# Decoding float64 weights with a parametric Relu, and splitting them on GpSimd, in a fused attention and MoE kernel

## The chip, the cores and the metric

The kernel runs on one core of a Trainium2 chip. The metric is the device time of one execution in microseconds (us). The core has five engines with instruction queues of their own, each worked off in order: TensorE (PE, with its weight loads shown apart as PEld), VectorE (DVE), ScalarE (ACT), GpSimd (POOL) and SyncE (SP, which issues the DMAs here). An instruction that has to wait holds up everything behind it in its own queue.

## The reference

Two layers in a row, without biases. For 8 batches and 8 heads with 576 positions and head size 64, thresholded softmax attention; then, on the 4608 tokens of width 512, a two-layer perceptron with SiLU.

```python
scores = q @ k.T / sqrt(64)
scores = where(scores >= max(scores) - tau, scores, -1e9)
attn = softmax(scores); x = attn @ v            # heads side by side: 4608 x 512
h = x @ w_in                                    # 512 x 2048
out = (h * sigmoid(h)) @ w_out                  # 2048 x 512
```

`q`, `k`, `v` are float32. `w_in` and `w_out` come as float64 numbers.

## The kernel before

**Weights.** They are loaded as pairs of 32-bit words, in 32 pieces of 128 x 512 (16 of `w_in`, then 16 of `w_out`). `decode_weights(i)` makes a float32 of each pair in the buffer `wst`. POOL multiplies the upper word, read as a float32, by 2^-112 (L179). DVE shifts the bits of this left by three (L183), which drops the sign, and ors in the top bits of the lower word (L186). PE multiplies a matrix of ones with the upper 16 bits of all four blocks of the piece (L197). The sums over four pieces bound the magnitudes, and DVE takes their maximum (L202). ACT makes the sign from the upper word (L204) and POOL multiplies it in (L205).

`pow2_scales` makes a power of two out of such bounds by a few operations on one column on DVE; for `v` it first takes the maximum over the partitions (a diagonal matrix by ACT, a matmul with ones on PE, a reduction on DVE). For the weights this was not needed, as the matmul with ones has already summed over the partitions. `split_weights(i)` then writes a high part in float16, scaled by ACT (L211), and a low part in float16, the scaled value less the high part, by DVE (L212). All this happens in one buffer: a split piece lies two slots ahead of the decoded one, so the high part of piece i may be written only once the split of piece i-2 has read its source.

**Attention.** A tile is 128 rows of scores. There are 288: first 16 of batch 0 (whose scores and products take float32 directly), then 20 of batch 0, then 36 for each further batch. Per tile PE makes the scores (L400 for the first 16, L412), DVE the maximum (L422), ACT the exponential (L432), DVE the threshold and the sum (L441), ACT the division (L454). For all but the first 16, the weights of the tile are split in two float16 parts: the high one by ACT, from the 9th of these tiles on by POOL (L465), the low one by POOL (L468 and L471); a DMA transposes them (`wT<-hl`), and PE multiplies them with `v` (L496). POOL also makes the low parts of the keys (`klo`, L326) and, in batch 0, of the queries (`qstack`, L311). The buffers of a tile's weights number four, those of its scores two, so a late step soon holds up the steps ahead of it.

**MoE.** `h_unit` (L539, 12 matmuls each) and `o_unit` (L570, 48 matmuls per output block) run on PE between the tiles. Each takes the high and the low part of the weights. A unit needs the weights' two parts, and the tokens' `x16`, made from the attention's output.

**What sets the order.** The program is written tile by tile, with a plan for the weights (`W_PLAN`: load, decode, scale, split at given tiles) and priorities. A scheduler then lays the instructions into the five queues by these priorities and by its own estimate of when each is ready. The order in the queues is fixed when the program is built. A change of one operation so moves others.

Of the kernel before, what the change touches and what calls it, by code (L numbers as in the profile page):

```python
# [52 lines left out]
def attention_moe(  # L53
# [51 lines left out]

    def pow2_scales(mx, name, across=True):

# [3 lines left out]
        nc.vector.tensor_reduce(out=one, in_=mx, op=ALU.max, axis=AX.X)  # L111
        if across:


            diag = const.tile([P, P], BF16, name=f"{name}_diag", tag="diag")
            nc.scalar.activation(diag, ident, AF.Copy, scale=one)
            allp = bank([P, P], f"{name}_ps", 0 if turn[1] == 3 else None)
            nc.tensor.matmul(allp, ones, diag, start=True, stop=True)
            one = const.tile([P, 1], F32, name=f"{name}_all", tag=f"{k}_all")
            nc.vector.tensor_reduce(out=one, in_=allp, op=ALU.max, axis=AX.X)  # L120
        cl = const.tile([P, 1], F32, name=f"{name}_cl", tag=f"{k}_cl")
        nc.vector.tensor_scalar(
            out=cl, in0=one, scalar1=2.0**-20, scalar2=2.0**47, op0=ALU.max, op1=ALU.min
        )
        e2 = const.tile([P, 2], I32, name=f"{name}_e2", tag=f"{k}_e2")
        nc.vector.tensor_scalar(
# [45 lines left out]
    def decode_weights(i):  # L172


        t = wraw.pop(i)
        low, top = t[:, :, 0], t[:, :, 1]
        w = wst[:, i + WSPARE, :]
        wbits = w.bitcast(I32)
        nc.gpsimd.tensor_scalar(  # L179
            out=w, in0=top.bitcast(F32), scalar1=2.0**-112, scalar2=1.0,  # L180
            op0=ALU.mult, op1=ALU.mult,
        )
        nc.vector.tensor_scalar(  # L183
            out=wbits, in0=wbits, scalar1=3, scalar2=None, op0=ALU.logical_shift_left
        )
        nc.vector.scalar_tensor_tensor(  # L186
            out=wbits, in0=low, scalar=29, in1=wbits,
            op0=ALU.logical_shift_right, op1=ALU.bitwise_or,
        )


        n, c = divmod(i, 4)
        if c == 0:
            wps[n] = bank([P, P], f"wps_{n}", 2)
        upper = w.bitcast(BF16).rearrange("p (c t) -> p c t", t=2)[:, :, 1]
        for j in range(4):
            nc.tensor.matmul(  # L197
                wps[n], ones, upper[:, j * P : (j + 1) * P],
                start=(c == 0 and j == 0), stop=(c == 3 and j == 3),
            )  # L200
        if c == 3:
            nc.vector.tensor_reduce(out=wmx[:, n : n + 1], in_=wps[n], op=ALU.max, axis=AX.X)  # L202
        sg = stage.tile([P, 512], F16, tag="wsg", name=f"wsg_{i}", bufs=2)
        nc.scalar.activation(sg, top.bitcast(F32), AF.Sign)  # L204
        nc.gpsimd.tensor_tensor(out=w, in0=w, in1=sg, op=ALU.mult)  # L205

    def split_weights(i):
        w = wst[:, i + WSPARE, :]
        hi = w16[:, i, 0:512]
        sc = wsc["in" if i < 4 * NK else "out"][:, 0:1]  # L210
        nc.scalar.activation(hi, w, AF.Copy, scale=sc)  # L211
        nc.vector.scalar_tensor_tensor(  # L212
            out=w16[:, i, 512:1024], in0=w, scalar=sc, in1=hi, op0=ALU.mult, op1=ALU.subtract
        )
# [33 lines left out]
    def vscale(b):  # L248
        vsc[b] = pow2_scales(vmx[b], f"v{b}")
        if b == 0:  # L250
# [430 lines left out]
    def scale_in():  # L681
        wsc["in"] = pow2_scales(wmx[:, 0:4], "i_w", across=False)

    def scale_out():
        wsc["out"] = pow2_scales(wmx[:, 4:8], "o_w", across=False)

# [128 lines left out]
```

## Time and profile before

The time is 1250.52 us, the median of three runs (1245.27 to 1252.15). One execution was profiled.

| | |
|---|---|
| profiled execution | 1244.94 us |
| its span, first to last instruction | 1243.2 us |
| PE busy | 1140.7 us (92%) |
| DVE busy | 961.3 us (77%) |
| ACT busy | 818.0 us (66%) |
| POOL busy | 759.4 us (61%) |
| mean granted PE clock | 0.971 |

Busy shares are averages over stages of different kinds. The weights are handled in the first 190 us; the last 180 us have no attention any more. In the profile, a row of a group gives line, engine, operation, `out<-in`, the shapes, the count, the busy time in us with the mean of one in ns, and the engine's idle time just ahead of these instructions with what ended it. A row of a stretch gives its bounds and length, the busy time and count of each engine, the granted clock, the share of time that the DMA engines were busy and their GB/s.

### The profile page before, as it was taken

To read this page: it belongs to the slowest core of one execution; us is meant where nothing else is said; L and a number is where in the kernel's file an instruction comes from. 1 tells how busy PE (TensorE), PEld (TensorE's weight loads), DVE (VectorE), ACT (ScalarE), POOL (GpSimd) and SP (SyncE) were. 2 spreads that over 40 slices of the span, in tenths; PEclk is the share of its full clock that TensorE was granted. 3 is DMA by queue.
4 is the path that set the end of the run, shared out by engine and by line. 5 is a ranking of instruction groups with operands and counts; after the bars stand their busy time and mean duration, and the time that the engine had idled before them with its cause. 6 is when DMAs were issued, how large, how long until landed. Compare 5 with 4: busy or idle time off the path is not lost.

```text
span 1243.2 us, 26997 instructions
## 1 busy us (share of the span) xinstructions
PE 1140.7 (92%) x9400; PEld 897.4 (72%) x9400; DVE 961.3 (77%) x2627; ACT 818.0 (66%) x1505; POOL 759.4 (61%) x952
## 2 busy tenths in 40 slices
PE   5674879899799989999999999999999999999998
PEld 3453657676577767777888877787777877777777
DVE  7999998978888888989888957988689848333230
ACT  5787777766777667777777747776577847433331
POOL 4568988577778768786878708773688538200000
PEclk8996889899899999999999999999999999999999
DMA  9457867678868868888778638783687436200000
GB/s 297 127 177 179 186 130 146 132 151 167 151 130 145 166 133 147 148 158 172 143 140 152 137 90 154 143 148 101 110 168 148 87 73 116 54 15 16 12 14 24
DMA packets 363480, 158.15 MB, mean 127 GB/s; under 512 B 329552, under 2 KB 338256, under 8 KB 363344
## 3 DMA queue, kind: packets, MB, share of 16 engines
q1 hardware_dynamic: 363344, 156.43, 61.9%
q8 instruction: 74, 1.21, 0.4%
q14 instruction: 62, 0.51, 0.1%
HBM read 66.72 MB, written 9.44 MB: 61 GB/s over the span
## 4 chain that ended last, share of the span: by engine, by line
PE 54%; DVE 25%; DMA 6%; ACT 6%; issue 5%; POOL 4%; SPq 0%; ACTq 0%; POOLq 0%; DVEq 0%
PE o L570 20%; PE h L539 19%; PE s L412 7%; PE a L496 7%; DVE w L441 6%; DVE sm L422 5%; DMA vraw<-in_vL 3%; DVE qstack L316 3%; ACT w L432 2%; DMA wT<-hl 2%; DVE wst L212 2%; DVE h L548 1%; DVE gbuf L555 1%; ACT w L454 1%; DVE wst L186 1%
## 5 line engine op out<-in xcount | busy, mean ns | idle before, releaser
L539 PE MATMUL h<-x,wst 128*128 128x288 f16 (+2 forms) x3072 | 430.8, 290 | 12.7 <-DVE gbuf L555 10.2
L570 PE MATMUL o<-gbuf,wst 128*128 128x288 f16 (+2 forms) x3072 | 420.6, 287 | 8.2 <-ACT wst L580 6.5
L539 PEld LDWEIGHTS <-wst 128*128 128x128 f16 x3072 | 294.6, 99 | 102.0 <-issue 22.0
L570 PEld LDWEIGHTS <-wst 128*128 128x128 f16 x3072 | 293.2, 98 | 90.5 <-issue 11.4
L468 POOL TENSOR_TENSOR hl<-w,hl 128x512 f16<-128x512 f32 x272 | 329.3, 1211 | 14.5 <-ACT hl L463 2.1
L465 POOL TENSOR_SCALAR hl<-w 128x576 f16<-128x576 f32 x264 | 180.6, 687 | 190.8 <-ACT w L454 128.3
L432 ACT ACTIVATE w<-s,sm 128x576 f32<-128x576 f32 x288 | 210.5, 738 | 83.5 <-DVE sm L422 30.6
L441 DVE SCALAR_TENSOR_TENSOR w<-s,sm,w 128x576 f32<-128x576 f32 x288 | 232.0, 812 | 32.5 <-ACT w L432 30.2
L454 ACT ACTIVATE w<-w,sm 128x576 f32<-128x576 f32 x288 | 217.6, 770 | 52.4 <-DVE sm L449 49.3
L422 DVE TENSOR_REDUCE sm<-s 128x1 f32<-128x576 f32 x288 | 215.0, 749 | 31.9 <-PE s L412 28.2
L548 DVE SCALAR_TENSOR_TENSOR h<-th,h 128x288 f32<-128x288 f32 (+2 forms) x256 | 116.2, 455 | 108.5 <-ACT th L547 106.4
L547 ACT ACTIVATE th<-h,msc 128x288 f32<-128x288 f32 (+2 forms) x256 | 126.2, 497 | 106.0 <-PE h L539 104.7
L412 PE MATMUL s<-khi,qstack 128*128 128x288 f32 x608 | 158.7, 343 | 19.0 <-DVE w L441 14.5
L554 ACT ACTIVATE gbuf<-h 128x288 f16<-128x288 f32 (+2 forms) x256 | 103.5, 407 | 81.3 <-DVE h L548 80.2
L555 DVE SCALAR_TENSOR_TENSOR gbuf<-h,gbuf 128x288 f16<-128x288 f32 (+2 forms) x256 | 114.9, 451 | 40.4 <-ACT gbuf L554 39.6
L496 PE MATMUL a<-wT,v 128*64 128x288 f16 (+1 forms) x1680 | 131.3, 298 | 13.5 <-DMA wT<-hl 13.3
L412 PE MATMUL s<-klo,qstack 128*128 128x288 f32 x608 | 132.6, 300 | 0.0
L326 POOL TENSOR_TENSOR klo<-kraw,khi 128x576 fp32r<-128x576 f32 x64 | 95.2, 1487 | 56.5 <-ACT khi L324 53.8
L412 PEld LDWEIGHTS s<-khi,qstack 128*128 128x128 f32 x608 | 97.9, 196 | 41.9 <-issue 22.9
L496 PEld LDWEIGHTS <-v 128*64 128x64 f16 x1680 | 94.5, 113 | 40.1 <-issue 30.3
L412 PEld LDWEIGHTS s<-klo,qstack 128*128 128x128 f32 x608 | 100.3, 194 | 0.3
L471 POOL TENSOR_TENSOR hl<-w,hl 128x64 f16<-128x64 f32 x272 | 100.2, 368 | 0.0
(84 smaller groups left out, 866.5 us busy)
## 6 DMA issues: line engine op xcount, KB each, us to landing
qraw<-in_qT SPq DMA_DIRECT2D x128, 144.0 KB, 3.0
kraw<-in_kT SPq DMA_DIRECT2D x128, 144.0 KB, 3.0
vraw<-in_vL SPq DMA_DIRECT2D x32, 320.0 KB, 3.7
wraw<-in_w_out SPq DMA_DIRECT2D x16, 512.0 KB, 3.8
out_t<-wst SPq DMA_DIRECT2D x56, 144.0 KB, 2.2
wT<-hl SPq DMA_TRANSPOSE x304, 3.4
gbuf<-in_w_in SPq DMA_DIRECT2D x8, 512.0 KB, 7.5
wraw<-in_w_in SPq DMA_DIRECT2D x8, 512.0 KB, 6.0
```

Of the source, the lines that this page charges most:

```text
L412: nc.tensor.matmul(s_ps[:, j, :HALF], lhs, kk[:, j * HALF : (j + 1) * HALF], start=(n == 0), stop=(n == len(seq) - 1),)
L422: nc.vector.tensor_reduce(out=negm, in_=s_ps[:, :, :HALF], op=ALU.max, axis=AX.XY, negate=True)
L432: nc.scalar.activation(wtile[t].rearrange("p (j c) -> p j c", j=2), sps[t][:, :, :HALF], AF.Exp, bias=small[t][:, 0:1],)
L441: nc.vector.scalar_tensor_tensor(out=w3, in0=s_ps[:, :, :HALF], scalar=sm[:, 1:2], in1=w3, op0=ALU.is_ge, op1=ALU.mult, accum_out=sm[:, 2:3],)
L454: nc.scalar.activation(w, w, AF.Copy, scale=r)
L465: nc.gpsimd.tensor_scalar(out=fl[:, 0:S], in0=w, scalar1=1.0, scalar2=1.0, op0=ALU.mult, op1=ALU.mult)
L468: nc.gpsimd.tensor_tensor(out=fl[:, 640:1152], in0=w[:, 0:512], in1=fl[:, 0:512], op=ALU.subtract)
L496: nc.tensor.matmul(a_ps[odd * D : (odd + 1) * D, :n], vt[:, lo_v, odd, kv, :], wT[v, b * H + 2 * p + odd][:, kw, c0 - base : c0 - base + n ...
L539: nc.tensor.matmul(ph[:, :n], wi(c, f, lo_w), x16[b, lo_x][:, c, c0 : c0 + n], start=(k == 0), stop=(k == 11),)
L548: nc.vector.scalar_tensor_tensor(out=ph[:, :n], in0=th[:, :n], scalar=1.0, in1=ph[:, :n], op0=ALU.add, op1=ALU.mult,)
L555: nc.vector.scalar_tensor_tensor(out=g[:, 1, :n], in0=ph[:, :n], scalar=2.0**-14, in1=g[:, 0, :n], op0=ALU.mult, op1=ALU.subtract,)
L570: nc.tensor.matmul(ps[:, :n], wo(f, d, lo_w), g[:, lo_g, :n], start=(f == 0 and k == 0), stop=(f == NF - 1 and k == 2),)
```

## The change

The decode: ACT applies a parametric Relu to the upper word with scale 2^-112 and slope 2^32 for negative numbers. After it a negative number has a larger exponent than a positive one, such that the shift by three leaves the sign bit in place. ACT's Sign and POOL's two operations are gone; DVE's two stay.

The bound: since the values now bear a sign, PE multiplies each block with itself, transposed, instead of with ones. The maximum of the sums is taken, now over the partitions too, and its root is made by halving the exponent. So the two scales of the weights go through the diagonal, the matmul and the reduction, and through three more one-column operations.

The split: POOL scales the piece in place (L220 of the changed kernel), ACT copies the high part (L223), POOL subtracts it (L224). DVE's L212 is gone. The PSUM banks of some of the scale matmuls are others.

```diff
-    def pow2_scales(mx, name, across=True):
+    def pow2_scales(mx, name, own=None, squared=False):
...
-        if across:
-            (the five statements below, indented)
+        diag = const.tile([P, P], BF16, name=f"{name}_diag", tag="diag")
+        nc.scalar.activation(diag, ident, AF.Copy, scale=one)
+        allp = bank([P, P], f"{name}_ps", own)
+        nc.tensor.matmul(allp, ones, diag, start=True, stop=True)
+        one = const.tile([P, 1], F32, name=f"{name}_all", tag=f"{k}_all")
+        nc.vector.tensor_reduce(out=one, in_=allp, op=ALU.max, axis=AX.X)
...
+        if squared:
+            nc.vector.tensor_scalar(out=twice, in0=cl, scalar1=2.0, scalar2=None, op0=ALU.mult)
+            nc.vector.tensor_scalar(
+                out=half, in0=twice.bitcast(I32), scalar1=1, scalar2=EXPMASK,
+                op0=ALU.logical_shift_right, op1=ALU.bitwise_and,
+            )
+            nc.vector.tensor_scalar(
+                out=cl, in0=half.bitcast(F32), scalar1=2.0**64, scalar2=None, op0=ALU.mult
+            )
...
     def decode_weights(i):
-        nc.gpsimd.tensor_scalar(
-            out=w, in0=top.bitcast(F32), scalar1=2.0**-112, scalar2=1.0,
-            op0=ALU.mult, op1=ALU.mult,
+        nc.scalar.activation(
+            w, top.bitcast(F32), AF.Prelu, scale=2.0**-112, alpha=2.0**32
         )
...
         for j in range(4):
+            part = upper[:, j * P : (j + 1) * P]
             nc.tensor.matmul(
-                wps[n], ones, upper[:, j * P : (j + 1) * P],
+                wps[n], part, part,
...
-        sg = stage.tile([P, 512], F16, tag="wsg", name=f"wsg_{i}", bufs=2)
-        nc.scalar.activation(sg, top.bitcast(F32), AF.Sign)
-        nc.gpsimd.tensor_tensor(out=w, in0=w, in1=sg, op=ALU.mult)

     def split_weights(i):
-        nc.scalar.activation(hi, w, AF.Copy, scale=sc)
-        nc.vector.scalar_tensor_tensor(
-            out=w16[:, i, 512:1024], in0=w, scalar=sc, in1=hi, op0=ALU.mult, op1=ALU.subtract
+        nc.gpsimd.tensor_scalar(
+            out=w, in0=w, scalar1=sc, scalar2=1.0, op0=ALU.mult, op1=ALU.mult
+        )
+        nc.scalar.activation(hi, w, AF.Copy)
+        nc.gpsimd.tensor_tensor(
+            out=w16[:, i, 512:1024], in0=w, in1=hi, op=ALU.subtract
         )
...
-        vsc[b] = pow2_scales(vmx[b], f"v{b}")
+        vsc[b] = pow2_scales(vmx[b], f"v{b}", (None, 2)[b] if b < 2 else 0)
...
-        wsc["in"] = pow2_scales(wmx[:, 0:4], "i_w", across=False)
+        wsc["in"] = pow2_scales(wmx[:, 0:4], "i_w", squared=True)
...
-        wsc["out"] = pow2_scales(wmx[:, 4:8], "o_w", across=False)
+        wsc["out"] = pow2_scales(wmx[:, 4:8], "o_w", 2, squared=True)
```

**How the order moves.** Lines of the changed kernel from L114 on stand at most 12 lines lower. POOL's queue from its first work on the weights, before (L179 and L205 are the decode, L311 the queries' low part):

```order
L179 TENSOR_SCALAR wst<-gbuf 128x512 x2
L205 TENSOR_TENSOR wst<-wst,wsg_147 128x512
L179 TENSOR_SCALAR wst<-gbuf 128x512 x2
L179 TENSOR_SCALAR wst<-wraw_160 128x512
L205 TENSOR_TENSOR wst<-wst,wsg_157 128x512
L179 TENSOR_SCALAR wst<-wraw_222 128x512
```

and the same place in the changed program (L323 are the queries, L338 the keys, L220 the scaling and L224 the subtraction of the split, `hl_1305` the first attention tile that POOL handles, number 28 of the program):

```order
L323 TENSOR_TENSOR qstack_85<-qraw_0_1047,qstack_85 64x320
L323 TENSOR_TENSOR qstack_87<-qraw_1_1118,qstack_87 64x320
L338 TENSOR_TENSOR klo_1116<-kraw_0_1048,khi_1114 128x576
L338 TENSOR_TENSOR klo_1203<-kraw_1_1119,khi_1201 128x576
L220 TENSOR_SCALAR wst<-wst,i_w_sc 128x512 x15
L224 TENSOR_TENSOR wst<-wst 128x512
L220 TENSOR_SCALAR wst<-wst,i_w_sc 128x512
L224 TENSOR_TENSOR wst<-wst 128x512
L338 TENSOR_TENSOR klo_1353<-kraw_2_1243,khi_1351 128x576
L323 TENSOR_TENSOR qstack_85<-qraw_2_1242,qstack_85 64x320
L480 TENSOR_TENSOR hl_1305<-w_28_1230,hl_1305 128x512
```

POOL has only four instructions on queries and keys until the scale of `w_in` is there, and then 15 scalings in one go, ahead of the first attention tile.

POOL's queue again, in the changed program, where the scale of `w_out` is ready (`hl_1888` and `hl_1927` are tiles 40 and 41):

```order
L477 TENSOR_SCALAR hl_1888<-w_40_1806 128x576
L338 TENSOR_TENSOR klo_1934<-kraw_7_1826,khi_1932 128x576
L323 TENSOR_TENSOR qstack_87<-qraw_7_1825,qstack_87 64x320
L477 TENSOR_SCALAR hl_1927<-w_41_1878 128x576
L220 TENSOR_SCALAR wst<-wst,o_w_sc 128x512 x15
L224 TENSOR_TENSOR wst<-wst 128x512
L220 TENSOR_SCALAR wst<-wst,o_w_sc 128x512
L224 TENSOR_TENSOR wst<-wst 128x512
L480 TENSOR_TENSOR hl_1888<-w_40_1806,hl_1888 128x512
L483 TENSOR_TENSOR hl_1888<-w_40_1806,hl_1888 128x64
```

Before, one decode multiplication stood between the tiles here, and no scaling; now 18 instructions of the split stand ahead of the low parts of tiles 40 and 41. The other 14 subtractions follow one or two at a time between later tiles.

PE's queue at the score of the 45th scored tile (tile 57), before (L412 the score, L570 the second layer, `o_0_3` the fourth and last output block of batch 0's first columns):

```order
L570 LDWEIGHTS wst
L570 MATMUL o_0_3_1938<-gbuf,wst 128x256
L412 MATMUL s_2437<-khi_2226,qstack_87 128x288 x2
L412 MATMUL s_2437<-klo_2228,qstack_87 128x288 x2
L570 LDWEIGHTS wst
L570 MATMUL o_0_3_1938<-gbuf,wst 128x256
```

and in the changed program (L424 the score, L582 the second layer):

```order
L582 LDWEIGHTS wst
L582 MATMUL o_0_1_1580<-gbuf,wst 128x256
L424 MATMUL s_2397<-khi_2186,qstack_87 128x288 x2
L424 MATMUL s_2397<-klo_2188,qstack_87 128x288 x2
L582 LDWEIGHTS wst
L582 MATMUL o_0_0_1444<-gbuf,wst 128x256
```

At the same tile PE is now still at the first two output blocks instead of the fourth. Counted over the queues, the old one has 166 matmuls of L570 ahead of this score, the new one 82 of L582; at the 85th scored tile they differ by 12 matmuls of the first layer and no more.

More of the change, by code (lines that the diff above doesn't have):

```diff
@@ L111, in pow2_scales @@
         nc.vector.tensor_reduce(out=one, in_=mx, op=ALU.max, axis=AX.X)
-        if across:
[L115 to L120, printed above, removed]
+        diag = const.tile([P, P], BF16, name=f"{name}_diag", tag="diag")
[4 more added lines that the diff above has]
+        nc.vector.tensor_reduce(out=one, in_=allp, op=ALU.max, axis=AX.X)
         cl = const.tile([P, 1], F32, name=f"{name}_cl", tag=f"{k}_cl")
+        low, high = (2.0**-40, 2.0**94) if squared else (2.0**-20, 2.0**47)
         nc.vector.tensor_scalar(
-            out=cl, in0=one, scalar1=2.0**-20, scalar2=2.0**47, op0=ALU.max, op1=ALU.min
+            out=cl, in0=one, scalar1=low, scalar2=high, op0=ALU.max, op1=ALU.min
         )
+        if squared:
+            twice = const.tile([P, 1], F32, name=f"{name}_twice", tag=f"{k}_twice")
+            nc.vector.tensor_scalar(
+                out=twice, in0=cl, scalar1=2.0, scalar2=None, op0=ALU.mult
+            )
+            half = const.tile([P, 1], I32, name=f"{name}_half", tag=f"{k}_half")
+            nc.vector.tensor_scalar(
+                out=half, in0=twice.bitcast(I32), scalar1=1, scalar2=EXPMASK,
+                op0=ALU.logical_shift_right, op1=ALU.bitwise_and,
+            )
+            cl = const.tile([P, 1], F32, name=f"{name}_root", tag=f"{k}_root")
+            nc.vector.tensor_scalar(
+                out=cl, in0=half.bitcast(F32), scalar1=2.0**64, scalar2=None, op0=ALU.mult
+            )
         e2 = const.tile([P, 2], I32, name=f"{name}_e2", tag=f"{k}_e2")
@@ L210, in split_weights @@
         sc = wsc["in" if i < 4 * NK else "out"][:, 0:1]
-        nc.scalar.activation(hi, w, AF.Copy, scale=sc)
-        nc.vector.scalar_tensor_tensor(
-            out=w16[:, i, 512:1024], in0=w, scalar=sc, in1=hi, op0=ALU.mult, op1=ALU.subtract
+        nc.gpsimd.tensor_scalar(
+            out=w, in0=w, scalar1=sc, scalar2=1.0, op0=ALU.mult, op1=ALU.mult
+        )
+        nc.scalar.activation(hi, w, AF.Copy)
+        nc.gpsimd.tensor_tensor(
+            out=w16[:, i, 512:1024], in0=w, in1=hi, op=ALU.subtract
         )
```

## The prediction

> **What bounds the kernel now.** I began with the busy time of each engine in five stretches of the span. The columns are stretch, length, then busy time and instruction count of PE, weight load, DVE, ACT and POOL, then granted clock, DMA share and GB/s.
>
> ```profile
> 0.00:75.00 75.00, 46.47 (x245) 29.82 (x245) 63.82 (x157) 51.10 (x95) 40.23 (x46) 0.93 0.66 207
> 75.00:190.00 115.00, 79.67 (x574) 61.91 (x574) 113.26 (x259) 91.13 (x168) 94.42 (x95) 0.82 0.69 163
> 206.00:215.00 9.00, 8.29 (x65) 6.30 (x64) 8.70 (x29) 6.73 (x11) 7.65 (x11) 1.00 0.87 174
> 215.00:345.00 130.00, 110.75 (x849) 84.64 (x851) 113.24 (x319) 90.29 (x159) 93.90 (x120) 0.92 0.77 152
> 345.00:1243.00 898.00, 879.57 (x7525) 700.69 (x7521) 650.32 (x1835) 568.85 (x1058) 509.11 (x664) 1.00 0.59 112
> ```
>
> From 345 us on PE is busy 98% of the time at full clock. The work left there is the same in both programs, so the change can act only ahead of it, where PE idles 28.5 us before 75 us, 35.3 us from 75 to 190 us and 20 us from 206 to 345 us. From 75 to 190 us DVE is busy 113.26 of 115 us: it bounds that stage. POOL is second, with 94.42.
>
> Then the chain of waits, in pieces (start, length, what), of the end of that stage and what follows:
>
> ```profile
> 183.01 0.66 DVE wst L212
> 189.16 1.47 POOL hl L468
> 195.70 1.36 POOL klo L326
> 197.06 1.64 POOL hl L468
> 200.83 1.33 POOL hl L465 x2
> 209.49 1.37 POOL klo L326
> ```
>
> DVE's weight split (L212) lies on the chain until about 185 us; from 189 us POOL does. So POOL is already the next bound, before anything is moved to it.
>
> **DVE's part.** The rows of single lines give shortest, median and longest duration in ns:
>
> ```profile
> L212 DVE SCALAR_TENSOR_TENSOR wst<-wst,i_w_sc x16: 734/1002/1643, 80.6 to 125.0; 128x512 f16<-128x512 f32 x16
> 75.00:190.00 115.00, 32.56 (x32) 0.82 0.69 163
> L183 DVE TENSOR_SCALAR wst<-wst x32: 400/848/1623, 12.0 to 151.8; 128x512 int32<-128x512 int32 x32
> 0.00:75.00 75.00, 14.00 (x18) 0.93 0.66 207
> 37.03 0.41 DVE L183 TENSOR_SCALAR wst<-wst 128x512 int32<-128x512 int32 x1
> 39.63 0.41 DVE L183 TENSOR_SCALAR wst<-wst 128x512 int32<-128x512 int32 x1
> L186 DVE SCALAR_TENSOR_TENSOR wst<-wraw,wst x24: 662/687/1451, 22.7 to 153.3; 128x512 int32<-128x512 int32 x24
> 0.00:75.00 75.00, 14.25 (x17) 0.93 0.66 207
> 44.83 1.16 POOL L205 TENSOR_TENSOR wst<-wst,wsg 128x512 f32<-128x512 f32 x1 [8.40 <-PE wps L197]
> L122 DVE TENSOR_SCALAR i_w_cl<-i_w_one x1: 135/135/135, 74.3 to 74.3; 128x1 f32<-128x1 f32 x1
> L120 DVE TENSOR_REDUCE v_all<-v_ps 128x1 f32<-128x128 f32 x3 | 0.8, 279 | 0.0
> ```
>
> (The first stretch row is L212's, the second L183's, the third L186's.) All 32 executions of L212, 32.56 us, leave DVE. The two scale chains add each a reduction over the partitions (279 ns) and three one-column operations (some 140 ns, as the 135): together 1.4 us.
>
> A second gain is indirect. L183 takes 0.41 us at 37 and 39 us, when POOL is idle (its 8.4 us pause ends at 44.83), but 0.78 us on average over the 18 before 75 us, and up to 1.62 us beside a busy POOL. In the changed program POOL has four small jobs before the first scale, so these 18 would take 0.41: 6.6 us less. L186 likewise falls from 0.84 to 0.68 us: 17 x 0.16 = 2.7 us. The first scale was ready at about 75.2 us (74.3 plus four operations and what stands between them). Now: 75.2 - 9.3 + 0.7 for the longer chain + 1.1 for one more decode that the order puts ahead (0.41 + 0.68) = 67.7 us, if DVE sets the pace; if loads or ACT do and the chain waits for its ACT and PE steps, nothing is won and it is about 78. I take 70, near the first end, since DVE is busy 85% there.
>
> The GPSIMD Engine Reference of the Trainium skill, section "Key points", says that GpSimd shares its SBUF interfaces with VectorE and contends with its two-port modes and its instructions with two SBUF inputs. The trace agrees by L183's 0.41 against 0.78 us; without it the scale would stand near 77 us and the sum below would end 7 us later.
>
> **POOL's part.** Two operations per weight leave, two come. Kinds and durations (first the single-line rows, then means of groups, over the first 330 us, in which DVE's traffic is included):
>
> ```profile
> L179 POOL TENSOR_SCALAR wst<-wraw x24: 646/844/1163, 17.9 to 150.9; 128x512 f32<-128x512 f32 x24
> L205 POOL TENSOR_TENSOR wst<-wst,wsg x32: 1152/1162/1615, 13.9 to 162.6; 128x512 f32<-128x512 f32 x32
> L468 POOL TENSOR_TENSOR hl<-w,hl x272: 1145/1160/1868, 93.9 to 1063.9; 128x512 f16<-128x512 f32 x136
> L471 POOL TENSOR_TENSOR hl<-w,hl x272: 294/306/891, 95.0 to 1065.1; 128x64 f16<-128x64 f32 x136
> L465 POOL TENSOR_SCALAR hl<-w x264: 660/670/1263, 133.0 to 1063.2; 128x576 f16<-128x576 f32 x132
> L326 POOL TENSOR_TENSOR klo<-kraw,khi x64: 1396/1410/1976, 62.8 to 1032.9; 128x576 fp32r<-128x576 f32 x64
> L311 POOL TENSOR_TENSOR qstack<-qraw,qstack x8: 860/866/1202, 31.4 to 156.3; 64x320 fp32r<-64x320 f32 x8
> L468 POOL TENSOR_TENSOR hl<-w,hl 128x512 f16<-128x512 f32 x62 | 76.5, 1233 | 4.9 <-ACT hl L463 2.1
> L205 POOL TENSOR_TENSOR wst<-wst,wsg 128x512 f32<-128x512 f32 x32 | 40.0, 1255 | 22.5 <-PE wps L197 12.6 <-ACT wsg L204 4.9 <-ACT wT L368 2.8
> L471 POOL TENSOR_TENSOR hl<-w,hl 128x64 f16<-128x64 f32 x61 | 26.2, 429 | 0.0
> ```
>
> The sum hardly changes: L179 and L205 go, 32 scalings (nearest row L179) and 32 subtractions (nearest L468, same shapes) come. What changes is when: the old pair ran from 11 to 163 us, beside the decode; the new one cannot start before the scale, and comes in two bursts of 15 and more, the second ahead of hl 40 and 41.
>
> So I follow POOL's queue from the first scale to the point just ahead of the 45th scored tile, whose score before was issued here:
>
> ```profile
> 205.62 0.51 PE L412 MATMUL s<-khi,qstack 128*128 128x288 f32 x2
> 206.23 3.01 PE L570 MATMUL o<-gbuf,wst 128*128 128x256 f16 x26
> ```
>
> The new order has 32 scalings, 30 subtractions, 9 klo, 6 qstack, 24 hl pairs and 17 hl copies up to there, 142 instructions. At the undisturbed durations (0.65, 1.16, 1.41, 0.87, 1.16 + 0.31, 0.67) that is 120 us; at durations stretched by DVE (0.83, 1.26, 1.51, 0.95, 1.23 + 0.43, 0.72) 136 us. Starts follow each other some 0.04 us before the end of the one ahead, which takes off 6: 114 to 130. I take 122, since L212, which had two SBUF inputs, is gone, but decode and qstack are still there. POOL idled 20.6 us from 75 to 190 us; with the longer queue I allow 5 (0 to 12). So 70 + 122 + 5 = 197 us, against 205.6: **8.6 us earlier**; the bounds are 182 and 220.
>
> A rule of the skill speaks against this step: the same page, section "Engine selection", puts two-input elementwise work on VectorE since GpSimd is about twice as slow. The rows say 1.16 against 0.73 us at the shortest; with twice 0.73 the 30 subtractions would cost 9 us more, which gives the first rival.
>
> **PE's part.** PE does less by then: ahead of the 45th score the old order has 166 matmuls of the second layer, the new 82, and 3 more of the first. At 3.01 us for 26 this is 84 x 0.116 - 3 x 0.14 = 9.3 us of work put off to tiles 75 to 85, where both orders are level again. From 206 to 345 us PE idles 20 us, so I book the deferred work as hidden there; without that cover it costs 9.3 us. What waits: PE's queue is in order, so the score of each next tile stands behind second-layer matmuls that wait for a subtraction of POOL, and DVE's softmax behind that score. This is counted in POOL's 197.
>
> **Edits at no cost.** On ACT the Prelu takes Sign's place over the same 512 columns and the copy of the high part loses its pointer:
>
> ```profile
> L204 ACT ACTIVATE wsg<-wraw 128x512 f16<-128x512 f32 x24 | 15.9, 667 | 7.4 <-DMA wraw<-in_w_out 6.3 <-POOL wst L205 1.1
> L211 ACT ACTIVATE wst<-wst,i_w_sc 128x512 f16<-128x512 f32 x16 | 11.4, 721 | 4.7 <-DVE wst L212 4.6
> L349 ACT ACT_TABLE_LOAD x1 | 1.3, 1283 | 4.5 <-DMA gbuf<-in_qT 4.5
> L197 PEld LDWEIGHTS <-ones x128: 95/96/207, 9.7 to 154.9; 128*128 128x128 bf16 x128
> ```
>
> ACT is not the bound (91 of 115 us), so 32 x (0 to -0.1) us is nothing; were Prelu as slow as 0.77 instead of 0.67, 3 us more would lie beside DVE and POOL. The built order has one table load, as before; reloads around each of 32 Prelus would have cost 64 x 1.28 = 82 us. The bound's 128 matmuls load the weights themselves: from no gain to a doubled load (128 x 0.096 = 12 us) under PE's 64 us of idle time before 190 us. The two added scale matmuls are under 0.5 us.
>
> **Sum.** The profiled execution took 1244.94 us (span 1243.2); less 8.6 this is 1236. The profiled one lies 5.6 us below the median of the runs, so against the median: 1250.5 - 8.6 = **1242 us**.
>
> **Rivals.**
>
> *POOL becomes the bound and is later than DVE was.* Place: its queue between the first scale and the last second-layer subtraction. With the scale at 74 us, 130 us of stretched work and 8 of idle, the 45th score comes at 212, 6 late; if half the deferred work finds no idle time, 4.6 more: 1261 us. It decides once start, work and idle together pass 205.6 us. For it: POOL's place on the chain after 189 us. Against: L212, the disturber, leaves.
>
> *The gain is eaten by the deferred matmuls.* 8.6 earlier, 9.3 paid in full: 1251 us. For it: PE's idle in 206 to 345 us comes in waits on softmax and transposes, which an in-order queue need not fill.
>
> *DVE's whole saving arrives.* The 45th score at 182 us, 23.6 earlier, deferred work hidden: 1227 us. Against: POOL's queue would have to run undisturbed and without a gap.
>
> **How the numbers follow.** Chances: forecast 0.46 (own range 1234 to 1250), POOL late 0.18, gain eaten 0.26, all of DVE's saving 0.10. The forecast's own bounds come from POOL's idle and durations, 8 us either way. A measurement of this kernel tells about 0.5%, 6.3 us, from no change, so faster means below 1244.3: four fifths of the forecast, all of the third rival, a little of the second: 0.49. Slower means above 1256.8: most of the first rival and a little of the second: 0.18. The rest, 0.33, is within. The range of 1229 to 1257 leaves out half of the first rival and about half of the third.
>
> **What would show it.** Right: L183 near 0.41 us before the first scale and that scale by 70 us; DVE clearly under full from 75 to 190 us; POOL nearly without idle there and on the chain; the 45th score near 197 us; less PE idle from 206 to 345 us. Wrong: the scale later than 75 us, POOL's subtractions above 1.3 us, PE or ACT waiting long for POOL's wst, the 45th score after 206 us, or a second table load.

## The result and the profile after

The changed kernel takes 1241.38 us (median of 7 runs, 1239.22 to 1242.44) against 1247.29 us of the kernel before beside it (7 runs): a ratio of 0.9947, 95% interval 0.9930 to 0.9964, 5.9 us less. The interval leaves out 1, so this is a gain, but a small one of about half a per cent. 1242 us was forecast. The profiled execution took 1240.96 us, its span 1238.8 us; before, 1244.94 and 1243.2.

The number came out, but the way to it did not. These are the stretches of the changed kernel, with the columns of the prediction's first table (stretch, length, busy time and count of PE, weight load, DVE, ACT and POOL, granted clock, DMA share, GB/s):

```profile
0.00:75.00 75.00, 52.99 (x292) 35.45 (x292) 64.26 (x185) 58.69 (x110) 13.52 (x21) 0.95 0.77 242
75.00:190.00 115.00, 74.77 (x516) 56.95 (x515) 88.89 (x231) 83.08 (x155) 107.43 (x120) 0.83 0.71 151
206.00:215.00 9.00, 6.68 (x33) 4.76 (x33) 6.02 (x16) 6.17 (x11) 8.74 (x11) 0.69 0.46 95
215.00:345.00 130.00, 121.33 (x1003) 93.31 (x1002) 111.65 (x322) 93.95 (x166) 99.16 (x130) 0.98 0.80 152
345.00:1239.00 894.00, 875.92 (x7485) 697.72 (x7483) 649.04 (x1823) 562.86 (x1051) 503.73 (x656) 1.00 0.58 112
67.50:203.30 135.80, 91.10 (x632) 69.46 (x631) 105.11 (x270) 99.07 (x185) 128.23 (x144) 0.84 0.70 153
```

Read them stage by stage. Before 75 us POOL has almost nothing to do any more (13.52 us, before 40.23), and PE gets 6.5 us more work done. From 75 to 190 us the bound has changed sides: DVE fell from 113.26 to 88.89 us, POOL rose from 94.42 to 107.43, and PE did 4.9 us *less* than before. From 215 to 345 us PE did 10.6 us more than before. Between these rows, from 190 to 206 us, POOL is busy without a gap and PE works 11.16 of 16 us, where before it worked all 16. From 345 us on little differs but the 3.65 us of PE work that have been done earlier, and this is about what the profiled execution gained (3.98 us).

The last row is POOL's queue as the prediction followed it, from the first scale to just ahead of the 45th score: 128.23 us of work in 135.8 us, so 7.6 us idle. (The row counts two instructions more than the prediction's 142, which reach over its edges.) The chain of waits of the changed kernel (start, length, what) tells the same:

```profile
142.02 7.97 POOL wst L220 x11
151.93 1.87 POOL wst L220 x2
153.79 1.12 POOL wst L224
155.59 1.12 POOL wst L224
156.70 1.12 POOL hl L480
208.66 1.16 POOL wst L224
210.43 1.66 POOL hl L480
217.63 4.98 DMA wT<-hl
```

Where DVE's split stood on the chain, POOL's scalings now stand, and the attention's low parts (`hl`, L480) come behind them. In the timeline the scalings of `w_out` are one block, and the 45th score comes as late as before (205.62 us):

```profile
142.00 11.79 POOL L220 TENSOR_SCALAR wst<-wst,o_w_sc 128x512 f32<-128x512 f32 x15
205.53 0.82 PE L424 MATMUL s<-khi,qstack 128*128 128x288 f32 x2 [4.21 <-DVE w L453]
```

So 4 to 6 us were won, and none of it ahead of the 45th tile. PE's work (first number after the length) from there to 345 us, of the kernel before and then of the changed one:

```profile
205.50:345.00 139.50, 119.54 (x919) 91.43 (x918) 122.39 (x346) 97.02 (x169) 102.05 (x131) 0.93 0.78 153
```

```profile
205.50:345.00 139.50, 128.47 (x1034) 98.57 (x1035) 118.14 (x339) 100.32 (x176) 108.39 (x141) 0.96 0.77 148
```

PE idles 11.0 us there instead of 20.0. The single lines of the changed kernel (shortest, median and longest ns, then first and last start), with DVE's shift in the first 75 us as the second row:

```profile
L194 DVE TENSOR_SCALAR wst<-wst x32: 404/423/1369, 12.3 to 125.2; 128x512 int32<-128x512 int32 x32
0.00:75.00 75.00, 9.21 (x21) 0.95 0.77 242
L146 DVE TENSOR_SCALAR i_w_sc<-i_w_e x1: 144/144/144, 67.3 to 67.3; 128x1 f32<-128x1 f32 x1
L220 POOL TENSOR_SCALAR wst<-wst,i_w_sc x16: 682/696/1120, 68.0 to 80.9; 128x512 f32<-128x512 f32 x16
L224 POOL TENSOR_TENSOR wst<-wst x32: 1146/1158/1598, 79.8 to 208.7; 128x512 f16<-128x512 f32 x32
L117 DVE TENSOR_REDUCE v_all<-v_ps x8: 277/280/291, 21.3 to 980.9; 128x1 f32<-128x128 f32 x8
```

The first scale is there at 67.3 us, 8.8 us earlier than before (76.1). The last row leads to something that the prediction passed over: the scale of `v`. Its second execution, that of batch 1, moved by 74 us. This is it before, and then in the changed kernel:

```profile
210.90 0.28 DVE L120 TENSOR_REDUCE v_all<-v_ps 128x1 f32<-128x128 f32 x1
```

```profile
136.85 0.28 DVE L117 TENSOR_REDUCE v_all<-v_ps 128x1 f32<-128x128 f32 x1
```

The change gives this scale's matmul bank 2 of the PSUM, which up to there only the weights' bound and `w_out`'s scale use, in place of one from a rotation of banks 0 and 1 that all units of batch 0's MoE share. Among DVE's instructions this reduction stood behind 45 tile maxima, and now it stands behind 31. This edit is "the bank" below; the expectations call it a bank of its own.

So there were three suspects for the 5.9 us, each of which could have gained or cost: the decode (with its bound, which no run takes apart from it), the split, and this bank.

### The profile page after: what moved, and what is told of

It reads as the page before. It is cut to its first block, busy times and chain, and to the rows that moved or that the text cites. A ratio compares the mean times of both kernels' runs of the same rounds, so it can differ in the third digit from the quotient of the medians.

```text
span 1238.8 us, 26929 instructions
## 1 busy us (share of the span) xinstructions
PE 1142.8 (92%) x9402; PEld 896.8 (72%) x9402; DVE 931.1 (75%) x2603; ACT 814.8 (66%) x1507; POOL 748.6 (60%) x952
## 3 DMA queue, kind: packets, MB, share of 16 engines
q8 instruction: 74, 1.21, 0.4%
## 4 chain that ended last, share of the span: by engine, by line
PE 64%; DVE 13%; DMA 8%; POOL 5%; ACT 5%; issue 3%; SPq 1%; POOLq 0%; ACTq 0%; DVEq 0%
PE h L551 23%; PE o L582 23%; PE s L424 10%; PE a L508 8%; DMA wT<-hl 3%; DVE w L453 3%; DVE sm L434 3%; DMA vraw<-in_vL 2%; DVE qstack L328 2%; POOL hl L480 2%; ACT w L444 2%; DVE v L289 1%; DMA wraw<-in_w_out 1%; POOL hl L477 1%; ACT w L466 1%
## 5 line engine op out<-in xcount | busy, mean ns | idle before, releaser
L582 PE MATMUL o<-gbuf,wst 128*128 128x288 f16 (+2 forms) x3072 | 426.2, 288 | 4.9 <-ACT wst L592 2.5
L582 PEld LDWEIGHTS <-wst 128*128 128x128 f16 x3072 | 294.5, 99 | 89.5 <-issue 9.1
L480 POOL TENSOR_TENSOR hl<-w,hl 128x512 f16<-128x512 f32 x272 | 325.3, 1196 | 15.7 <-DMA kraw<-in_kT 3.5
L424 PE MATMUL s<-khi,qstack 128*128 128x288 f32 x608 | 160.6, 346 | 31.3 <-DVE w L453 27.2
L508 PE MATMUL a<-wT,v 128*64 128x288 f16 (+1 forms) x1680 | 128.7, 295 | 10.2 <-DMA wT<-hl 10.2
L424 PEld LDWEIGHTS s<-khi,qstack 128*128 128x128 f32 x608 | 98.6, 197 | 53.8 <-issue 42.1
L338 POOL TENSOR_TENSOR klo<-kraw,khi 128x576 fp32r<-128x576 f32 x64 | 92.5, 1446 | 71.3 <-ACT khi L336 71.3
L424 PE MATMUL s<-klo,qstack 128*128 128x288 f32 x608 | 133.7, 302 | 0.0
L508 PEld LDWEIGHTS <-v 128*64 128x64 f16 x1680 | 91.3, 111 | 37.0 <-issue 25.0
L424 PEld LDWEIGHTS s<-klo,qstack 128*128 128x128 f32 x608 | 101.5, 196 | 0.5 <-issue 0.2
```

The source lines that it names most:

```text
L424: nc.tensor.matmul(s_ps[:, j, :HALF], lhs, kk[:, j * HALF : (j + 1) * HALF], start=(n == 0), stop=(n == len(seq) - 1),)
L480: nc.gpsimd.tensor_tensor(out=fl[:, 640:1152], in0=w[:, 0:512], in1=fl[:, 0:512], op=ALU.subtract)
L508: nc.tensor.matmul(a_ps[odd * D : (odd + 1) * D, :n], vt[:, lo_v, odd, kv, :], wT[v, b * H + 2 * p + odd][:, kw, c0 - base : c0 - base + n ...
L582: nc.tensor.matmul(ps[:, :n], wo(f, d, lo_w), g[:, lo_g, :n], start=(f == 0 and k == 0), stop=(f == NF - 1 and k == 2),)
```

## The experiments

All times are medians beside runs of the kernel before on the same chip (1245.1 to 1246.7 us); ratios are against those. The medians of the kernel before differ by up to 2.2 us between these sets of runs and those of the result (1247.29 us), so variants from different sets are better compared by their ratios; where it matters I give both. "45th tile" is the moment at which DVE starts the 45th of the tiles' maxima in the trace (before 206.4 us, changed 206.9 us), and "45 to 60" the time from there to the 60th (57.4 and 47.8 us).

### The two halves apart

The kernel before with only the split moved to POOL (decode, bound and banks as before):

```diff
-        nc.scalar.activation(hi, w, AF.Copy, scale=sc)
-        nc.vector.scalar_tensor_tensor(out=w16[:, i, 512:1024], in0=w, scalar=sc, in1=hi, ...)
+        nc.gpsimd.tensor_scalar(out=w, in0=w, scalar1=sc, scalar2=1.0, op0=ALU.mult, op1=ALU.mult)
+        nc.scalar.activation(hi, w, AF.Copy)
+        nc.gpsimd.tensor_tensor(out=w16[:, i, 512:1024], in0=w, in1=hi, op=ALU.subtract)
```

> Kernel before with only the split moved (POOL scales in place, ACT copies the high part, POOL subtracts); decode, sign pass and bound stay as before. Theory A (from the first weight scale on POOL's queue sets the pace): POOL keeps its 66 us of decode and gets some 60 us of split on top, so by the 45th scored tile it has over 205 us of work: that score comes 10 to 25 us later than before's 205.6 us and the time is 5 to 20 us longer than before. Rival B (what counts is that DVE loses L212's 32.6 us): 5 to 20 us shorter than before, like the whole change or better.

And the changed kernel with the split of the kernel before, the same lines the other way round:

> The changed kernel with the split of before (ACT scales into the high part, DVE's scalar_tensor_tensor makes the low part). Theory A: POOL loses 66 us and nothing comes back; the first scale comes at 67 to 70 us as in the changed kernel; L212's counterpart falls from 1.02 to some 0.75 us because POOL is quieter, so DVE's stage from 75 to 190 us shrinks by about 10 us; the 45th score at 190 to 198 us and the time 5 to 12 us shorter than before, so at least as good as the whole change. Rival B (the gain is L212's leaving DVE): within 2 us of before.

Measured: the split alone **1278.85 us**, ratio 1.0271 (1.0243 to 1.0299). The decode, with the new bank, and the old split **1232.87 us**, ratio 0.9890 (0.9869 to 0.9910). The half that was to bring the gain costs 32 us, which is in the direction of theory A but beyond its 5 to 20 us, and the other half alone brings more than the whole change does: 13.9 us, a little more than the 5 to 12 expected. Two details of the second expectation were missed: the split on DVE fell to 0.75 us at the median only and not on average, as its rows (shortest, median and longest ns, then a group's busy time and mean) show, and the 45th tile came only 2.8 us earlier (203.6).

```profile
L221 DVE SCALAR_TENSOR_TENSOR wst<-wst,i_w_sc x16: 739/745/1656, 73.5 to 106.9; 128x512 f16<-128x512 f32 x16
L221 DVE SCALAR_TENSOR_TENSOR wst<-wst,i_w_sc 128x512 f16<-128x512 f32 x16 | 13.9, 873 | 0.3 <-ACT wst L220 0.2
75.00:190.00 115.00, 78.35 (x555) 60.71 (x553) 105.88 (x274) 90.55 (x167) 65.49 (x73) 0.81 0.69 159
```

The stretch row shows what this kernel has that neither of the others has: DVE 9 us below full *and* POOL at 65 of 115 us. Of the split alone, the stretch from 190 to 206 us, ahead of its 45th tile at 223.1 us (theory A had it 10 to 25 us later, and it is 16.7):

```profile
190.00:206.00 16.00, 5.67 (x24) 3.49 (x24) 5.07 (x16) 5.83 (x10) 16.00 (x25) 0.57 0.14 21
```

POOL is busy without a gap, and PE, DVE and ACT are each idle for about two thirds of the time. But in that kernel the scale of `v` had also slipped, to 271 us, so it did not yet show that POOL's load alone costs the 32 us.

### Which part of the split costs: the scaling, or one of the two weights

The changed kernel, scaling in place on DVE and subtracting on POOL:

```diff
-        nc.gpsimd.tensor_scalar(
+        nc.vector.tensor_scalar(
             out=w, in0=w, scalar1=sc, scalar2=1.0, op0=ALU.mult, op1=ALU.mult
```

> The changed kernel, but the scaling in place is done by DVE (tensor_scalar, some 0.42 us) instead of POOL (0.69 us and more); POOL keeps the subtraction. Theory A: POOL's queue from the scale to the 45th score loses 32 x 0.7 = 22 us and DVE, which has 26 us to spare from 75 to 190 us, takes 13: the 45th score at 190 to 197 us instead of 205.5, the time 3 to 9 us shorter than the changed kernel's (1232 to 1238). Rival B (DVE's load sets the pace): 3 to 8 us longer than the changed kernel's.

And the changed kernel in which the pieces of `w_out` are split as before (ACT and DVE), those of `w_in` by POOL:

```diff
+        if i < 4 * NK:
             (the three statements of the change)
+        else:
+            nc.scalar.activation(hi, w, AF.Copy, scale=sc)
+            nc.vector.scalar_tensor_tensor(out=w16[:, i, 512:1024], in0=w, scalar=sc, in1=hi, ...)
```

> The changed kernel, but the 16 pieces of w_out are split as before (ACT scaled, DVE subtracts), those of w_in by POOL. Theory A: POOL's second burst (15 scalings at 142 us, 12 us) and its 16 subtractions go, so that POOL no longer sets the pace after 140 us: the 45th score at 188 to 197 us, time 3 to 9 us shorter than the changed kernel's. Rival C (the changed kernel gains because second-layer matmuls are put off into PE's idle time after 206 us, and an earlier 45th score is worth nothing): within 2 us of the changed kernel's or longer, as fewer are put off (103 instead of 83 ahead of the 45th score).

Scaling on DVE: **1240.09 us**, 0.9943 (0.9922 to 0.9964), no different from the whole change, and the 45th tile later (214.9). Neither theory's numbers held. The two rows of DVE's scaling suggest one reason. The median is not far from the 0.42 us that I had counted on by the shift's rows, but the longest are three times as long, and the means are 0.83 and 0.89 us: the scalings run while POOL subtracts the pieces ahead. POOL's subtraction got longer too, as the third row shows, with a median of 1.28 us against 1.16 in the changed kernel. That these longer durations are what ate the gain was not shown.

```profile
L220 DVE TENSOR_SCALAR wst<-wst,i_w_sc x16: 472/476/1376, 69.2 to 83.3; 128x512 f32<-128x512 f32 x16
L220 DVE TENSOR_SCALAR wst<-wst,o_w_sc x16: 474/500/1627, 151.4 to 163.9; 128x512 f32<-128x512 f32 x16
L224 POOL TENSOR_TENSOR wst<-wst x32: 1144/1283/1717, 71.0 to 194.2; 128x512 f16<-128x512 f32 x32
```

`w_out` back on DVE: **1232.60 us**, 0.9879 (0.9857 to 0.9900), the 45th tile at 198.5, a little later than theory A's 188 to 197. Rival C is out. This is the time of the kernel with no split on POOL at all (1232.87). So to move `w_in`'s whole split is worth nothing, and once it has moved, moving `w_out`'s whole split as well costs 8.8 us. Its 15 scalings in a row (11.79 us) stand ahead of the attention's low parts in the chain above. `w_out`'s split alone on POOL was not run.

### The bank of v's second scale

The kernel before with only this bank changed:

```diff
-            allp = bank([P, P], f"{name}_ps", 0 if turn[1] == 3 else None)
+            allp = bank([P, P], f"{name}_ps", own)
...
-        vsc[b] = pow2_scales(vmx[b], f"v{b}")
+        vsc[b] = pow2_scales(vmx[b], f"v{b}", own=(None, 2)[b] if b < 2 else 0)
```

> The kernel before with nothing but the PSUM bank of the scale of v for batch 1 changed (its matmul takes bank 2, as in the changed kernel, and not the next of the two banks that the MoE units use); decode, split and weight bound as before. Theory D (before, this scale's matmul could not get a bank until 209 us, since the second layer's sums held both; four splits of v then crowd DVE from 215 to 220 us, and PE idles beside): the stretch from the 45th to the 60th tile shrinks from 58 to about 49 us, and the time is 4 to 9 us shorter than before (1238 to 1243). Rival A (the bank is of no consequence; what gained was that POOL lost the decode): within 2 us of before.

And the whole change without it:

```diff
-        vsc[b] = pow2_scales(vmx[b], f"v{b}", (None, 2)[b] if b < 2 else 0)
+        vsc[b] = pow2_scales(vmx[b], f"v{b}", None if b < 2 else 0)
```

> The changed kernel with nothing but the bank of that scale set back to the next of the two banks of the MoE units; decode, bound and split are those of the change. Theory D: the scale of v for batch 1 comes after 200 us again, tiles 45 to 60 take 55 us or more, and the time is 4 to 9 us longer than the changed kernel's (1245 to 1250), so that without the bank the change is no gain. Rival A: within 2 us of the changed kernel's 1241.

The bank alone: **1246.10 us**, 1.0012 (0.9997 to 1.0026). Tiles 45 to 60 took 49.4 us, 8.0 less, as theory D expected, but the 45th came 11.0 us later (217.4), and the time is that of rival A. The whole change without the bank: **1247.94 us**, 1.0011 (0.9996 to 1.0026). This is what theory D expected: without the bank the change gains nothing. The scale then came here, and in the chain of waits `v`'s splits on DVE (L289) follow in a cluster:

```profile
230.48 0.28 DVE L117 TENSOR_REDUCE v_all<-v_ps 128x1 f32<-128x128 f32 x1
```

```profile
235.06 1.25 DVE v L289
236.44 0.78 DVE v L289
237.96 1.76 DVE v L289 x2
```

Up to the 45th tile this kernel and the changed one are nearly level (205.4 and 206.9), but its tiles 45 to 60 take 55.2 us instead of 47.8, and from 205.5 to 345 us PE does the old amount:

```profile
205.50:345.00 139.50, 119.60 (x954) 91.61 (x952) 121.15 (x334) 96.46 (x167) 104.60 (x133) 0.94 0.79 154
```

119.6 us as in the kernel before (119.54), against 128.47 in the changed one. That is where the change's gain came from. One thing the two runs don't separate: a matmul that is given its bank by number doesn't advance the rotation (`bank()` in the kernel), so that the units of batch 0 behind it get the other of the two banks.

### A busy POOL beside the decode

The changed kernel with two more POOL operations for each of the 16 pieces of `w_in`, of the size of the two that the decode had before, with a float16 output. Nothing else reads what they write.

```diff
+        if i < 4 * NK:
+            junk = stage.tile([P, 512], F16, tag="wsg", name=f"junk_{i}", bufs=2)
+            nc.gpsimd.tensor_scalar(out=junk, in0=top.bitcast(F32), scalar1=2.0**-112, ...)
+            nc.gpsimd.tensor_tensor(out=junk, in0=junk, in1=junk, op=ALU.mult)
```

> The changed kernel plus two idle operations on POOL for each of the 16 pieces of w_in (a scaling and a product, written to a scratch tile that nothing reads, of the sizes that the old decode had there). It puts back POOL's traffic ahead of the first scale and nothing else. Theory A: the shift operations on DVE go back from 0.44 to some 0.7 us, the first scale from 67.5 to 71 to 76 us, and since POOL is full from there on, the 45th score and the time follow by 3 to 7 us (1244 to 1248). Rival E (the moment of the first scale has slack): under 2 us longer.

**1248.02 us**, 1.0018 (1.0003 to 1.0033): 6.6 us more than the changed kernel by the medians (8.8 by the ratios), the first scale back at 76.2 us, and the 45th tile 8.7 us later (215.6). This is theory A, at the upper end of its numbers. In the first 75 us, all engines, and then the shift alone (busy time and count):

```profile
0.00:75.00 75.00, 47.60 (x251) 30.71 (x252) 66.02 (x161) 51.51 (x95) 37.54 (x43) 0.89 0.66 213
0.00:75.00 75.00, 12.97 (x19) 0.89 0.66 213
```

The mean of the shift before 75 us goes with POOL's busy time there: 0.42 us at 6.25 us (decode with the old split), 0.44 at 13.52 (changed), 0.68 at 37.54 (here), 0.78 at 40.23 (before). In all fourteen profiles it is 0.42 to 0.46 us where POOL is busy 6 to 14 us, and 0.68 to 0.83 us where it is busy 38 to 40 us. The GPSIMD Engine Reference of the Trainium skill, section "Key points", says that GpSimd shares its SBUF interfaces with VectorE and contends with those of its instructions that run in a two-port mode or have two SBUF inputs. The rows agree in that the shift gets longer beside a busy POOL; whether the shift, which has one input, runs in such a mode no run shows. What the run does not tell apart is DVE's longer operations from the places that the extra ones take in POOL's own queue: the 6.6 us are both together.

### The two corners that were missing

The split alone, now with bank 2 for `v`'s second scale (both edits above on the kernel before):

> The kernel before with only the split moved to GpSimd, and with v's second scale in the bank that the changed kernel gives it. The run of the split alone was 32 us slower, but there v's scale stood far behind the other work, after 250 us. Theory A (GpSimd, which keeps the decode's 64 operations here, becomes the bound): about as long again as its extra work, GpSimd above 110 us busy of 115 from 75 to 190 us, the 45th tile after 218 us and the time 10 to 35 us above the kernel before. Rival B (the 32 us were mostly the wait for v's scale): with the bank the time is within 5 us of the kernel before, and v's scale is made ahead of 170 us.

And the new decode and bound alone, with the old split and with the old rotation of banks:

> The new decode and bound alone: the split as in the kernel before (VectorE), and v's second scale in the rotation of banks. In the built order this scale then stands between the maxima of the 49th and 51st tile; with the bank of its own it stood after the 30th. It is the last corner of decode x split x bank. Theory A (the bank is worth its 6.6 us wherever the new decode is, the decode some 7 us by itself, the split on GpSimd costs 8.5): 1236 to 1241 us, tiles 45 to 60 above 52 us. Rival B (the decode alone brings all of the 12 to 14 us, the bank matters only beside the split on GpSimd): 1230 to 1234 us. Rival C (the bank carries all): 1244 to 1250 us.

Split with bank: **1285.77 us**, 1.0293 (1.0260 to 1.0326). The scale of `v` came at 186 us, not as early as the 170 of rival B, but 85 us earlier than in the split alone, and it did not help. The 45th tile came at 235.0 us. POOL's row is that of theory A, whose upper end of 35 us the 40.7 us even exceed:

```profile
75.00:190.00 115.00, 74.18 (x499) 54.55 (x496) 89.39 (x223) 78.11 (x148) 111.88 (x123) 0.78 0.65 158
190.00:206.00 16.00, 6.22 (x29) 4.03 (x26) 12.33 (x28) 7.62 (x14) 16.00 (x21) 0.61 0.41 96
```

Decode without bank: **1230.91 us**, 0.9878 (0.9859 to 0.9896). This is rival B: the decode brings all of it alone. `v`'s scale comes at 206 us, the 45th tile already at 192.0, and PE has less left to do after 345 us:

```profile
345.00:1300.00 955.00, 863.45 (x7353) 686.91 (x7351) 631.47 (x1787) 552.92 (x1029) 496.11 (x645) 1.00 0.54 103
```

863.45 us are 16.1 us less than the 879.57 before; by the medians 15.0 us were gained. With these the eight corners of the change are complete, as ratios to the kernel before:

| decode | split | v's scale in the rotation | in bank 2 |
|---|---|---|---|
| old | DVE | 1 | 1.0012 |
| old | POOL | 1.0271 | 1.0293 |
| new | DVE | 0.9878 | 0.9890 |
| new | POOL | 1.0011 | 0.9947 (the change) |

The three parts do not add up as terms. The decode gains 1.2% with the split on DVE and 2.5 to 3.4% with the split on POOL. The split on POOL costs 0.6 to 1.3% with the new decode, 2.7 to 2.8% with the old. The bank gains 0.6% in one corner of four, that of the change, and nothing that can be told apart in the others. Why only there was not settled, but the traces show part of it. In all four pairs the late scale leaves the four splits of `v` for batch 1 (DVE) between the 45th and the 60th tile, and the early one puts them ahead of the 45th. In all four pairs tiles 45 to 60 get shorter by that: 57.4 to 49.4 us (old decode, split on DVE), 73.5 to 56.6 (old, POOL), 52.2 to 46.7 (new, DVE), 55.2 to 47.8 (the change). But in the first three the 45th tile comes 11.0, 11.9 and 11.6 us later with it, and only in the change hardly so (1.5 us). What lets the change take these splits in at so small a price is open.

### How much of the split POOL can take

The changed kernel with every second piece split by POOL and the others as before:

```diff
+        if i % 2:
             (the three statements of the change)
+        else:
+            nc.scalar.activation(hi, w, AF.Copy, scale=sc)
+            nc.vector.scalar_tensor_tensor(out=w16[:, i, 512:1024], in0=w, scalar=sc, in1=hi, ...)
```

> The changed kernel with the even pieces split as before (ACT scaled, DVE subtracts) and the odd ones by POOL. Theory A (POOL's queue from the first scale on sets the pace of the whole change): POOL loses about 30 us between scale and 45th score, DVE takes 14: the 45th score at 195 to 201 us instead of 205.5, time 1230 to 1237 us, near the two runs with less split on POOL (1232.6, 1232.9). Rival C (it is by place, not by amount: only the second burst matters): within 3 us of the whole change, 1238 to 1244, since a half burst is still ahead of tiles 40 and 41.

Then the same with `if i % 4 == 1` (a quarter on POOL) and with `if i % 4` (three quarters):

> The changed kernel with every fourth piece split by GpSimd and the rest by VectorE as before. None on GpSimd gave 1232.9 us, every second 1225.2, all 1241.4. Theory A (the load of the two engines decides, which is balanced near one half): between the neighbours, 1226 to 1231 us, with VectorE at 105 us or more busy of 115 from 75 to 190 us. Rival B (the order that the scheduler happens to lay decides): outside 1224 to 1234 us.

> The changed kernel with three of four pieces split by GpSimd and the fourth by VectorE. Theory A (the load of the two engines decides): between 1225 and 1241 us, near 1230 to 1236, with GpSimd between its 95 us (one half) and 107 us (all) busy from 75 to 190 us. Rival B (the order decides): outside 1225 to 1241 us.

| share on POOL | us | ratio (95%) | DVE, POOL busy of 115 us (75 to 190) | PE busy from 345 us |
|---|---|---|---|---|
| 0 | 1232.87 | 0.9890 (0.9869 to 0.9910) | 105.88, 65.49 | 872.54 |
| 1/4 | 1227.65 | 0.9850 (0.9824 to 0.9876) | 111.04, 83.53 | 859.91 |
| 1/2 | **1225.22** | 0.9836 (0.9813 to 0.9858) | 107.16, 95.25 | 863.70 |
| 3/4 | 1233.66 | 0.9901 (0.9876 to 0.9926) | 102.64, 110.25 | 868.14 |
| 1 | 1241.38 | 0.9947 (0.9930 to 0.9964) | 88.89, 107.43 | 875.92 |

The rows of the half and of three quarters:

```profile
75.00:190.00 115.00, 84.53 (x565) 64.22 (x564) 107.16 (x271) 90.82 (x170) 95.25 (x100) 0.78 0.76 167
```

```profile
75.00:190.00 115.00, 79.86 (x594) 61.68 (x593) 102.64 (x268) 91.63 (x171) 110.25 (x120) 0.88 0.77 169
```

The half came out below the 1230 to 1237 us that theory A gave it, with the 45th tile where it was expected (195.8), and rival C is out. The quarter and the three quarters lie between their neighbours, as the balance of load would have it, though POOL at three quarters was busier than the 95 to 107 us that were expected. A quarter and a half cannot be told apart; half beats both kernels, the one before by 21 us and the changed one by 16 us (14 by the ratios). In the half PE has 84.53 us of work from 75 to 190 us, 9.8 more than with all of the split on POOL. Load is not all of it. POOL at three quarters is busier than with the whole split (107.43) and the kernel is still faster. The run with the scaling on DVE had DVE and POOL busy for 105.53 and 89.90 us, near the half's, and took 14.9 us more; there each piece passes through three engines one after the other, and whether that is the cause was not tried. The run with `w_out`'s split on DVE has nearly the half's load as well and took 7.4 us more:

```profile
75.00:190.00 115.00, 78.79 (x546) 60.31 (x547) 103.77 (x258) 89.81 (x166) 93.80 (x99) 0.79 0.70 156
```

So that an even load is the cause of the half's time is argued here and not shown; in the half the block of `w_out`'s scalings ahead of the attention's low parts is also shorter (8 in 6.96 us instead of 15 in 11.79).

## Why the prediction was right and where it was wrong

**What bounds the kernel: right.** The time followed the PE work left after 345 us: 863.70 us in the half, 875.92 in the changed kernel, 879.57 before, 912.23 in the split alone, for profiled executions of 1225.98, 1240.96, 1244.94 and 1276.69 us. The difference is 362 to 365 us in each of these, and 361 to 368 in all runs but the split with the bank (373). This spread is as large as the change's own gain, so the rule orders only the large differences.

**DVE's part: right in its numbers, wrong in what they are worth.** The shift fell to 0.44 us before 75 us (0.41 predicted), the scale came at 67.3 us (70 taken, 67.7 the early end, reckoned from an old scale at 75.2 us, which the trace has at 76.1), the 32.56 us left DVE. But L212's leaving, which was to free the stage, was no gain: leaving it on DVE beside the new decode saves 8.5 us (7.1 by the ratios). What I gave as the second, indirect gain, POOL silent during the decode, belongs to the part that is worth more: the decode alone brings 15 us, and 32 POOL operations of no use beside it, in the changed kernel, cost 6.6 us or more.

**POOL's part: the step that failed.** "So 70 + 122 + 5 = 197 us" became 67.5 + 128.2 + 7.6 = 203.3, within the bounds of 182 and 220. The 142 instructions took 128.2 us, not 122. I had taken the middle between undisturbed and stretched durations, less 6 us for the overlap of neighbours. The subtractions, at 1.19 us on average, kept to that middle (1.21). The 32 scalings took 0.80 to 0.81 us on average (middle 0.74), though their medians are 0.69 and 0.70, which makes 2.1 us; the 24 pairs of the attention's low parts took 40.2 us (middle 37.6); and the overlap was 4 us. With the other kinds near their middles the work came to 6.2 us more than taken. This and 2.6 us more of idle, less 2.5 for the earlier scale, put the end of this queue 6.3 us later than in the sum, and the score came 2.2 us later still: 205.53 against 205.62 before. The rule that I weighed against this step, that two-input work on GpSimd is about twice as slow (the Trainium skill, GPSIMD Engine Reference, section "Engine selection"), missed too: the subtraction's median is 1.158 us, as its row has it, not twice 0.73. Its advice to leave such work on VectorE was right here for the whole split, for another reason (POOL's full queue), and not for a quarter or a half of it.

**PE's part: right.** The deferred second-layer work was hidden where I booked it: PE did 8.9 us more from 205.5 to 345 us and idled 11.0 us there instead of 20.0, and the 85th tile came 7.3 us earlier (339.3 against 346.6), not later. The rival in which this work eats the gain did not come; but the cover was there only because of the next point.

**The edits at no cost: one was missing from the list.** The parametric Relu took 0.667 us as Sign did, there was one table load, and PE's own weight loads stayed at 0.097 us. The bank of `v`'s second scale was not priced at all. It is worth 6.6 us in this change by the medians (8.0 by the ratios), the whole of its gain: without it the time is 1247.94 us. With a lead of nothing at the 45th tile, the prediction's sum without this term gives no change, and that is what the run without the bank measured. So it was luck that the forecast of 8.6 us less came out near the measured 5.9: it rested on a lead that was not there and left out the gain that was.

**The rivals.** POOL late had the right place and the right direction (45th score no earlier), but not its 6 us of delay, nor its 1261 us. DVE's whole saving did not arrive, since POOL was the next bound, as I had read from the chain after 189 us.

## What to carry to other kernels

When work is moved from a full engine to the next fullest, price the receiver's queue with its durations under load, and ask whether half of it would do: here a share of one quarter to one half was worth 12 to 16 us over moving all. When several edits come together, find those that only change a bank or a buffer, and look where the built order puts what hangs on them; such a line can carry the whole result. And build the corners one by one before telling which part of a change brought what: here the part meant as the relief cost time, and the part that made room for it was the gain.

## What the runs showed of the hardware that I had not expected

- DVE's operations on one 128x512 piece stretch up to three or four times (the shift before: 0.40 us at the shortest, 1.62 at the longest), and the shift's mean goes with POOL's load: before 75 us it went from 0.42 to 0.78 us with POOL's busy time. The scaling on DVE took 0.48 us at the median and up to 1.63. The longest of both lie 1.2 us above the shortest, about the length of one POOL subtraction (1.16 us), as if the operation had waited for one; that it does was not shown. The split of `w_in` on DVE had a median of 0.75 us where POOL was busy 65 of 115 us, and 1.00 before, with POOL at 94. So a mean taken from one profile belongs to that profile's neighbours.
- POOL's operations stretch too, but not all alike. The subtraction of the same piece hardly moved in the changed kernel (median 1.16 us, mean 1.19), and had a median of 1.28 where DVE scaled the pieces beside it. The scalings took 0.69 to 0.70 us at the median and 0.80 to 0.81 on average, and the short operations of the attention's low parts 0.29 to 0.89 us:

```profile
L483 POOL TENSOR_TENSOR hl<-w,hl x272: 294/307/891, 87.3 to 1060.8; 128x64 f16<-128x64 f32 x136
```
